# Chunked RWKV attention and a SwiGLU block in fp32: one masked score product per head for a 128-step chunk, and float64 weights rounded 768 columns at a time

## The chip, the cores and the metric

The kernel runs on one core of a Trainium2 chip. A core has TensorE (matrix products and turns, called PE in the profile, with its weight loads as PEld), VectorE (DVE), ScalarE (ACT), GpSimd (POOL) and SyncE (SP), which issues most transfers here. Each engine works through its own instructions in order and waits on the others by semaphores. The metric is the device time of one execution in microseconds; the time before is the median of three runs.

## The reference

Attention by linear recurrence per batch and head (4 batches, 8 heads, 768 steps, 48 columns per head), then a SwiGLU feed-forward block over 3072 tokens:

```python
for t in range(S):
    kt, vt, rt = (k[:, :, t], v[:, :, t], r[:, :, t])
    cur = np.einsum('bhd,bhe->bhde', u[None] * kt, vt)
    y[:, :, t] = np.einsum('bhd,bhde->bhe', rt, state + cur)
    state = w[None, :, :, None] * state + np.einsum('bhd,bhe->bhde', kt, vt)
...
x = y.transpose(0, 2, 1, 3).reshape(B * S, H * D)       # 3072 x 384
g = x @ w_gate                                           # 384 x 1536
silu = g * (1.0 / (1.0 + np.exp(-g)))
out = (silu * (x @ w_val)) @ w_out                       # 1536 x 384
```

`r`, `k`, `v` and `u` are fp32; `w` is `rand * 0.1 + 0.85`; the three weight matrices reach the kernel as float64, seen as int64.

## The kernel before

A unit is one chunk of 128 steps of one batch, with all 8 heads; there are 24 units, unit `i` being chunk `i // 4` of batch `i % 4`. In the turned layout the heads lie in pairs, head 2a+e on partitions 64e to 64e+47 of column a.

Three kinds of work are put in order by hand.

- **Attention.** `prepare(i)` turns k and r by TensorE (L211), copies them out of PSUM (L215), and multiplies the turned tiles by powers of w: for each of six levels l a key part on VectorE (L229) and a row part on GpSimd (L233), both into `sc`. It also forms `rhat` (L240, VectorE), `khat` (L224, GpSimd), `rk` (L220, L221), `du` (L243) and `dv` (L245). `scores(i)` splits the pairs (j, t) of a chunk by the highest bit in which j and t differ: seven levels, each with four products per half of the heads (L259, 64 columns wide) and one predicated copy into the score tile `At` under that level's mask (L265). No negative power of w occurs. `products(i)` multiplies scores by v (L282) and the old state by `rhat` (L277), forms the state's update `u_ps` (L290), adds `dv` to give `xs` (L297) and renews the state (L305 to L308). `turn_x(i)` turns `xs` for the block (L317, L318).
- **Weight rounding.** 36 chunks of 128 x 384 are loaded as float64 bits, three ahead (L115), and rounded to fp32 by integer operations: five on VectorE (L131, L134 to L137) and four on GpSimd (L132, L133, L138, L140).
- **The block.** 256 tokens (two units) form a group `g`, of which there are 12. `gate_value(g, f)` makes gate and value of 128 of the 1536 columns (L331), then sigmoid (L336, ScalarE) and two products (L337, L338, VectorE). `project(g, j)` multiplies by `w_out` (L344), copies (L349) and stores.

Group 0 rounds three weight chunks in each `gate_value`. A queue `todo` holds the block's items; the attention's step `s` feeds two of them after each of its four parts:

```python
for s in range(N + 2):
    if s < N:
        prepare(s)
        ...
        feed(2)
    if 1 <= s <= N:
        scores(s - 1)
        feed(2)
    if s >= 2:
        products(s - 2)
        feed(2)
        turn_x(s - 2)
        if s % 2:
            queue((s - 2) // 2)
        feed(2)
```

Of the kernel before, what the change touches and what calls it, by code (L numbers as in the profile page):

```python
# [10 lines left out]
INT32 = mybir.dt.int32  # L11
AF = mybir.ActivationFunctionType
ALU = mybir.AluOpType
AX = mybir.AxisListType
P = 128


@with_exitstack
def kernel(
    ctx: ExitStack,  # L20
# [11 lines left out]
    """RWKV5 in chunks of 128 steps, then the SwiGLU block, all in fp32.  # L32

    The weights of the block come as the bits of float64, in int64 tensors, and
    are rounded to fp32 on the chip.

    A unit is one chunk of one batch with its 8 heads. In the turned layout the
    heads lie in pairs, head 2a+e at partitions 64e..64e+47 of column a.

    Within a chunk, y_t takes r_t * w^(t-1-j) * k_j for j < t. The pairs (j, t)  # L40
    are split by the highest bit l in which j and t differ: there t is in an odd
    block of 2^l steps and j in the even one before it, and the exponent is
    (t mod 2^l) + (2^l - 1 - j mod 2^l). Both parts are at least 0, so no power
    of w is ever divided by, and any w will do.
    """
# [10 lines left out]
    ctx.enter_context(tc.manual_schedule())  # L56
# [40 lines left out]
    # chunk f of wg and wv: columns 128f.. of all CC row blocks; chunk f of wo: rows 128f..  # L97
# [82 lines left out]
    # masks[j, l, (m i)]: j is in the even block before the odd block m of t  # L180
# [14 lines left out]
    for t in state:  # L195
        pool.memset(t[:], 0.0)

# [1 line left out]
    turned, scaled, rhat, khat, dvs, xs, xT = {}, {}, {}, {}, {}, {}, {}  # L199

    def blocks(t, l):
# [215 lines left out]
```

## Time and profile before

| | |
|---|---|
| median of 3 runs | 1161.31 us (1160.63 to 1161.44) |
| span of the profiled execution | 1158.1 us |
| TensorE, products | 1025.8 us (89%), 5964 instructions |
| TensorE, weight loads | 868.1 us (75%) |
| VectorE | 591.4 us (51%) |
| GpSimd | 340.3 us (29%) |
| ScalarE | 106.7 us (9%) |
| mean granted TensorE clock | 0.860 |
| read from HBM, written | 28.51 MB, 4.72 MB |

The page is one profiled execution; its own time is its span of 1158.1 us, from its first to its last instruction. The median of the timed runs stands 3.2 us above it. A row of instructions names line, engine, operation, output and inputs, the shape, how many there were, the time in which any of them ran, the mean of one in ns, and the engine's idle time ahead of them with what ended it. A row of the chain of work that ended last, or of a timeline, gives start and duration in us; rows of equal kind are merged (xN). A row of the windows view gives, for a stretch, each engine's busy us and instructions (TensorE, its weight loads, VectorE, ScalarE, GpSimd), then the granted TensorE clock as a share of full speed, the share of the DMA engines and GB/s. Matrix products overlap each other, so the mean duration of one is longer than the distance between two starts.

### The profile page before, as it was taken

The numbers are of one execution on the slowest core, as the hardware profiler recorded it, in microseconds if no ns is written. First come the engines' busy times: TensorE is split into PE (matmuls) and PEld (weight loads), VectorE is DVE, ScalarE is ACT, GpSimd is POOL, SyncE is SP. The second block draws the span as 40 slices with busy tenths as digits, with TensorE's granted clock in tenths as the row PEclk, the third lists the DMA queues.
The fourth block names the chain that finished last, engine by engine and source line by source line (L and its number), as shares of the span: only waits on it lengthen the run. The fifth ranks groups of instructions, "written<-read, shape, count | busy, mean of one in ns | idle before, by whom it ended". The sixth has DMA issues, their size and how long they took to land.

```text
span 1158.1 us, 14858 instructions
## 1 busy us (share of the span) xinstructions
PE 1025.8 (89%) x5964; PEld 868.1 (75%) x5964; DVE 591.4 (51%) x1108; ACT 106.7 (9%) x243; POOL 340.3 (29%) x416
## 2 busy tenths in 40 slices
PE   3577335369999999999999999999999999999998
PEld 3577334257887987987987887887887888878875
DVE  7877989993353353354354344344434524522211
ACT  1001000000011011001100100100100100100110
POOL 9644857872113113113122221211311212100000
PEclk9999757667879879879879879879978978988999
DMA  5212323311011011011011001101101100000000
GB/s 136 55 41 48 89 69 96 95 35 28 8 21 28 8 21 28 8 22 35 1 22 35 18 5 35 21 1 35 22 1 35 22 1 14 1 7 8 1 14 14
DMA packets 90292, 34.18 MB, mean 30 GB/s; under 512 B 76272, under 2 KB 88688, under 8 KB 90224
## 3 DMA queue, kind: packets, MB, share of 16 engines
q1 hardware_dynamic: 90224, 33.24, 11.5%
q8 instruction: 47, 0.77, 0.3%
q14 instruction: 21, 0.17, 0.0%
HBM read 28.51 MB, written 4.72 MB: 29 GB/s over the span
## 4 chain that ended last, share of the span: by engine, by line
PE 74%; DVE 23%; issue 2%; ACT 1%; DMA 0%; SPq 0%; POOL 0%; ACTq 0%; DVEq 0%; POOLq 0%
PE gv L331 30%; PE s_ps L259 19%; PE o_ps L344 16%; DVE sc L229 6%; PE y_ps L282 4%; DVE w_mt L134 3%; DVE w_ex L131 3%; DVE w_mt L135 2%; PE u_ps L290 2%; PE y_ps L277 2%; DVE sg L337 1%; DVE w_mt L136 1%; DVE hT L338 1%; DVE rhat L240 1%; DVE w_up L137 1%
## 5 line engine op out<-in xcount | busy, mean ns | idle before, releaser
L259 PE MATMUL s_ps<-sc 48*128 48x64 f32 x2304 | 250.2, 367 | 64.0 <-DVE At L265 64.0
L331 PE MATMUL gv<-xT,wg 128*128 128x256 f32 x864 | 253.8, 437 | 55.9 <-POOL w_mt L138 39.8
L259 PEld LDWEIGHTS s_ps<-sc 48*128 48x128 f32 x2304 | 243.6, 271 | 66.2 <-DVE At L265 66.1
L331 PEld LDWEIGHTS gv<-xT,wg 128*128 128x128 f32 x864 | 182.2, 220 | 90.6 <-POOL w_mt L138 51.9
L331 PE MATMUL gv<-xT,wv 128*128 128x256 f32 x864 | 232.7, 410 | 0.0
L265 DVE COPY_PREDICATED At<-masks,s_ps 128x256 f32<-128x256 int32 x336 | 157.1, 530 | 124.3 <-PE s_ps L259 122.2
L337 DVE TENSOR_TENSOR sg<-sg,gv 128x256 f32<-128x256 f32 x144 | 60.3, 419 | 287.1 <-ACT sg L336 287.0
L331 PEld LDWEIGHTS gv<-xT,wv 128*128 128x128 f32 x864 | 182.8, 212 | 30.8
L344 PE MATMUL o_ps<-wo,hT 128*128 128x384 f32 x576 | 189.8, 486 | 0.6 <-ACT o_sb L349 0.6
L233 POOL TENSOR_TENSOR sc<-rT,up 128x256 f32<-128x256 f32 x144 | 124.0, 892 | 205.7 <-ACT rT L215 205.7
L344 PEld LDWEIGHTS o_ps<-wo,hT 128*128 128x128 f32 x576 | 109.4, 190 | 72.4 <-ACT o_sb L349 1.2
L229 DVE TENSOR_TENSOR sc<-kT,down 128x256 f32<-128x256 f32 x144 | 109.8, 828 | 70.8 <-ACT kT L215 70.8
L307 POOL TENSOR_TENSOR state<-state,wL 64x192 f32<-64x192 f32 x32 | 16.1, 502 | 366.6 <-PE y_ps L277 365.4
L336 ACT ACTIVATE sg<-gv 128x256 f32<-128x256 f32 x144 | 55.2, 383 | 719.5 <-PE gv L331 719.5
L338 DVE TENSOR_TENSOR hT<-sg,gv 128x256 f32<-128x256 f32 x144 | 60.6, 421 | 4.9
L282 PE MATMUL y_ps<-v_ld,At 128*128 128x48 f32 x384 | 58.4, 284 | 0.0
L282 PEld LDWEIGHTS y_ps<-v_ld,At 128*128 128x128 f32 x384 | 54.6, 209 | 0.4
L259 PEld LDWEIGHTS s_ps<-rT,kT 48*128 48x128 f32 x384 | 38.9, 204 | 10.3 <-issue 9.6
L259 PE MATMUL s_ps<-rT,kT 48*128 48x64 f32 x384 | 42.4, 294 | 0.0
L138 POOL TENSOR_TENSOR w_mt<-w_mt,w_ex 128x384 int32<-128x384 int32 x36 | 35.8, 993 | 19.0 <-DVE w_mt L136 18.8
L134 DVE TENSOR_SCALAR w_mt<-w_bits 128x384 int32<-128x384 int32 x36 | 37.1, 1030 | 0.0
L297 DVE TENSOR_TENSOR xs<-y_ps,dv 128x384 f32<-128x384 f32 x24 | 13.4, 557 | 43.5 <-PE y_ps L282 43.5
(57 smaller groups left out, 581.1 us busy)
## 6 DMA issues: line engine op xcount, KB each, us to landing
k_ld<-in_k_dram SPq DMA_DIRECT2D x24, 192.0 KB, 2.7
r_ld<-in_r_dram SPq DMA_DIRECT2D x24, 192.0 KB, 3.3
v_ld<-in_v_dram SPq DMA_DIRECT2D x24, 192.0 KB, 3.5
w_bits<-in_moe_w_gate_dram SPq DMA_DIRECT2D x12, 384.0 KB, 3.2
w_bits<-in_moe_w_val_dram SPq DMA_DIRECT2D x12, 384.0 KB, 3.3
w_bits<-in_moe_w_out_dram SPq DMA_DIRECT2D x12, 384.0 KB, 3.0
out_dram<-o_sb SPq DMA_DIRECT2D x24, 192.0 KB, 1.9
ub<-in_u_dram SPq DMA_DIRECT2D x1, 192.0 KB, 4.4
```

Source lines behind the costliest of these rows:

```text
L134: dve.tensor_scalar(mt[:], hi, 3, 0x7FFFF8, ALU.logical_shift_left, ALU.bitwise_and)
L138: pool.tensor_tensor(mt[:], mt[:], ex[:], ALU.add)
L229: dve.tensor_mul(blocks(x[:], l)[:, :, :, 0, :], blocks(kT[:], l)[:, :, :, 0, :], down[:, :, P - n : P].unsqueeze(2).to_broadcast([P, HP, ...
L233: pool.tensor_mul(blocks(x[:], l)[:, :, :, 1, :], blocks(rT[:], l)[:, :, :, 1, :], up[:, :, 0:n].unsqueeze(2).to_broadcast([P, HP, 64 // n ...
L259: pe.matmul(s_ps[:, a, :], keys[p0:p1, a, :], rows[p0:p1, a, :].rearrange("p (m o i) -> p m o i", o=2, i=n)[:, :, 1, :], start=True, stop= ...
L265: dve.copy_predicated(blocks(A[:, e], l)[:, :, :, 1, :], mask.unsqueeze(1).to_broadcast([P, HP, 64 // n, n]), s_ps[:].rearrange("p a (m i) ...
L282: pe.matmul(y_ps[:, a, D * e : D * (e + 1)], A[:, e, a, :], vl[:, 2 * a + e, :], start=(c == 0), stop=True, skip_group_check=True,)
L331: pe.matmul(gv[:, o, :], wt[:, c, P * f : P * (f + 1)], xT[g][:, c, :], start=(c == 0), stop=(c == CC - 1),)
L336: act.activation(sg[:], gv[:, 0, :], AF.Sigmoid)
L337: dve.tensor_mul(sg[:], sg[:], gv[:, 0, :])
L338: dve.tensor_mul(hT[g][:, f, :], sg[:], gv[:, 1, :])
L344: pe.matmul(o_ps[:], hT[g][:, f, P * j : P * (j + 1)], wo[:, f, :], start=(f == 0), stop=(f == FC - 1),)
```

## The change

A new program `fast` stands ahead of the old one, which is kept as `general` and runs only if a number that the chip counts itself, of decays w outside 0.8 to 1.25, is above zero.

In `fast`, k is multiplied by w^(127-j) and r by w^(-(128-t)) before the turn, in the layout in which they are loaded, on GpSimd; both factors are tables (`kscale`, `rscale`) made in the set-up with one reciprocal and eight turns. One product per head then gives all scores of a chunk, 128 columns wide over 48 rows (8 products per unit instead of 56), and one predicated copy per half of the heads (2 instead of 14) takes the part j < t. The six levels' scale products are gone; the turned `rT` also meets the state, which is now a block-diagonal tile `Z` with w^128 folded in (`wL`), updated whole. v is stored in a zero-padded tile, so that the two heads of a pair accumulate into the same 96 columns. Step `s` prepares unit s+1, turns unit s, takes the scores of unit s-1 and the outputs and update of unit s-2, and turns the outputs of unit s-3.

Weights are rounded in 18 chunks of 128 x 768: two operations on ScalarE, two on VectorE, one on GpSimd; one chunk after the turn of a step and one at its end. The block's queue is fed in six places of a step, with no items up to step 3, three per step in steps 4 to 7, six in 8 and 9, and twelve from 10; `project` is cut into three parts that lie between `gate_value` items. The output's store is issued by ScalarE. Cut to its core:

```diff
+W_LOW, W_HIGH = 0.8, 1.25
...
+    two = ctx.enter_context(tc.tile_pool(name="two", bufs=2))
+    three = ctx.enter_context(tc.tile_pool(name="three", bufs=3))
+    ps_a = ctx.enter_context(tc.tile_pool(name="ps_a", bufs=5, space=bass.MemoryType.PSUM))
+    ps_f = ctx.enter_context(tc.tile_pool(name="ps_f", bufs=2, space=bass.MemoryType.PSUM))
+    ps_o = ctx.enter_context(tc.tile_pool(name="ps_o", bufs=1, space=bass.MemoryType.PSUM))
...
+    v_ld = [cst.tile([P, HP, 2, 2 * D], FP32, name=f"v_ld{i}") for i in range(4)]
+    khat = [cst.tile([P, H, DP], FP32, name=f"khat{i}") for i in range(4)]
+    rhat = [cst.tile([P, H, DP], FP32, name=f"rhat{i}") for i in range(2)]
+    At = [cst.tile([P, 2, HP, P], FP32, name=f"At{i}") for i in range(2)]
+    def v_heads(i):
+        t = v_ld[i % 4]
+        return [t[:, :, e, D * e : D * (e + 1)] for e in range(2)]
...
+    def load_v(i):
+        c, b = divmod(i, B)
+        rows = slice(P * c, P * (c + 1))
+        for e, dst in enumerate(v_heads(i)):
+            sp.dma_start(
+                out=dst, in_=v[b, :, rows, :].rearrange("(a e) t d -> e t a d", e=2)[e]
+            )
...
+    chunks = []
+    for f in range(FC // 2):
+        for src, dst in ((moe_w_gate, wg), (moe_w_val, wv)):
+            cols = slice(2 * P * f, 2 * P * (f + 1))
+            chunks.append((src[:, cols].rearrange("(c p) f -> p c f", p=P), dst[:, :, cols]))
+    for f in range(FC // 2):
+        chunks.append((
+            moe_w_out[2 * P * f : 2 * P * (f + 1)].rearrange("(c p) f -> p c f", p=P),
+            wo[:, 2 * f : 2 * f + 2, :],
+        ))
+    WN = 6 * P
+    AHEAD = 3
...
+    def round_weights(count):
+        for _ in range(count):
+            n = state["rounded"]
+            if n == len(chunks):
+                return
+            state["rounded"] += 1
+            x = bits.pop(n)
+            lo, hi = x[:, :, 0], x[:, :, 1]
+            dst = chunks[n][1].bitcast(INT32)
+            mag = two.tile([P, WN], INT32, name="w_mag", tag="w_mag")
+            low = two.tile([P, WN], INT32, name="w_low", tag="w_low")
+            act.activation(mag[:].bitcast(FP32), hi.bitcast(FP32), AF.Abs, scale=float(2.0**-112))
+            act.activation(low[:], lo.bitcast(UINT32), AF.Copy, scale=float(2.0**-29))
+            c = dst.shape[1]
+            mag, low, hi = (t.rearrange("p (c f) -> p c f", c=c) for t in (mag[:], low[:], hi))
+            dve.tensor_scalar(dst, hi, -(1 << 31), None, ALU.bitwise_and)
+            dve.scalar_tensor_tensor(dst, mag, 3, dst, ALU.logical_shift_left, ALU.bitwise_or)
+            pool.tensor_tensor(dst, dst, low, ALU.add)
+            load_weights()
...
+    make_identity(nc, ident[:])
+    dve.tensor_scalar(held[:], wcol[:], W_LOW, W_HIGH, ALU.max, ALU.min)
+    dve.tensor_copy(sq[:, 0, :], held[:])
+    for l in range(1, 8):
+        dve.tensor_mul(sq[:, l, :], sq[:, l - 1, :], sq[:, l - 1, :])
+    pw = two.tile([P, HP, P + 1], FP32, name="pw", tag="hT")
+    ipw = two.tile([P, HP, P], FP32, name="ipw", tag="hT")
+    dve.memset(pw[:, :, P : P + 1], 1.0)
+    dve.tensor_copy(pw[:, :, P - 1 : P], held[:].unsqueeze(2))
+    for l in range(7):
+        n = 1 << l
+        f = sq[:, l, :].unsqueeze(2).to_broadcast([P, HP, n])
+        dve.tensor_mul(pw[:, :, P - 2 * n : P - n], pw[:, :, P - n : P], f)
+    dve.reciprocal(ipw[:], pw[:, :, 0:P])
+    for src, dst in ((pw[:, :, 1 : P + 1], kscale), (ipw[:], rscale)):
+        t_ps = ps_a.tile([P, HP, P], FP32, name="t_ps", tag="a")
+        for a in range(HP):
+            pe.transpose(t_ps[:, a, :], src[:, a, :], ident[:])
+        act.copy(dst[:].rearrange("p h d -> p (h d)"), t_ps[:].rearrange("p a x -> p (a x)"))
+    pool.memset(wL[:], 0.0)
+    for e in range(2):
+        q = slice(64 * e, 64 * e + 64)
+        dve.tensor_copy(
+            wL[q, :, D * e : D * (e + 1)], sq[q, 7, :].unsqueeze(2).to_broadcast([64, HP, D])
+        )
+    pool.memset(mask[:], 1.0)
+    pool.affine_select(
+        out=mask[:], in_=mask[:], compare_op=ALU.is_gt, fill=0.0,
+        base=0, pattern=[[1, P]], channel_multiplier=-1,
+    )
+    for t in At:
+        pool.memset(t[:], 0.0)
+    dve.tensor_tensor(bad[:], held[:], wcol[:], ALU.not_equal)
+    dve.tensor_reduce(badc[:], bad[:], axis=AX.X, op=ALU.add)
+    dve.memset(ones[:], 1.0)
+    n_ps = ps_a.tile([P, HP, P], FP32, name="n_ps", tag="a")
+    pe.matmul(n_ps[0:1, 0, 0:1], badc[:], ones[:], start=True, stop=True)
+    act.copy(outside, n_ps[0:1, 0, 0:1])
...
+    def prepare(i):
+        kl, rl = k_ld[i % 2], r_ld[i % 2]
+        rk = two.tile([P, H, D], FP32, name="rk", tag="rk")
+        pool.tensor_mul(khat[i % 4][:], kl[:], kscale[:])
+        pool.tensor_mul(rhat[i % 2][:], rl[:], rscale[:])
+        pool.tensor_mul(rk[:], rl[:, :, 0:D], kl[:, :, 0:D])
+        pool.tensor_mul(rk[:], rk[:], ub[:])
+        du = three.tile([P, H], FP32, name="du", tag="du")
+        dve.tensor_reduce(du[:], rk[:], axis=AX.X, op=ALU.add)
+        dus[i] = du
+        load_v(i)
+        if i + 2 < N:
+            load(i + 2)
+    def turn(i):
+        got = []
+        for nm, t in (("kT", khat[i % 4]), ("rT", rhat[i % 2])):
+            tp = ps_a.tile([P, HP, P], FP32, name="tp", tag="a")
+            for a in range(HP):
+                pe.transpose(
+                    tp[:, a, :], t[:, 2 * a : 2 * a + 2, :].rearrange("p e d -> p (e d)"), ident[:]
+                )
+            x = (two if nm == "kT" else three).tile([P, HP, P], FP32, name=nm, tag=nm)
+            act.copy(x[:], tp[:])
+            got.append(x)
+        turned[i] = got
+    def scores(i, e):
+        kT, rT = turned[i]
+        q = slice(64 * e, 64 * e + D)
+        ps = ps_a.tile([P, HP, P], FP32, name="s_ps", tag="a")
+        for a in range(HP):
+            pe.matmul(
+                ps[:, a, :], kT[q, a, :], rT[q, a, :],
+                start=True, stop=True, skip_group_check=True,
+            )
+        dve.copy_predicated(
+            At[i % 2][:, e], mask[:].bitcast(INT32).unsqueeze(1).to_broadcast([P, HP, P]), ps[:]
+        )
+    def own(i):
+        du = dus.pop(i)
+        dvs[i] = two.tile([P, HP, 2, D], FP32, name="dv", tag="dv")
+        for e, vh in enumerate(v_heads(i)):
+            dve.tensor_mul(
+                dvs[i][:, :, e, :], vh,
+                du[:].rearrange("p (a e) -> p a e", e=2)[:, :, e : e + 1].to_broadcast([P, HP, D]),
+            )
+    def outputs(i):
+        c, b = divmod(i, B)
+        A, vl = At[i % 2], v_ld[i % 4]
+        rT = turned.pop(i)[1]
+        ps = ps_a.tile([P, HP, 2 * D], FP32, name="y_ps", tag="a")
+        for a in range(HP):
+            if c > 0:
+                pe.matmul(
+                    ps[:, a, :], rT[:, a, :], Z[b][:, a, :],
+                    start=True, stop=False, skip_group_check=True,
+                )
+            for e in range(2):
+                pe.matmul(
+                    ps[:, a, :], A[:, e, a, :], vl[:, a, e, :],
+                    start=(c == 0 and e == 0), stop=(e == 1), skip_group_check=True,
+                )
+        xs[i] = two.tile([P, DM], FP32, name="xs", tag="xs")
+        dve.tensor_add(
+            xs[i][:], ps[:].rearrange("p a x -> p (a x)"),
+            dvs.pop(i)[:].rearrange("p a e d -> p (a e d)"),
+        )
+    def update(i):
+        c, b = divmod(i, B)
+        if c == NCH - 1:
+            return
+        kh, vl, z = khat[i % 4], v_ld[i % 4], Z[b]
+        ps = ps_a.tile([P, HP, 2 * D], FP32, name="u_ps", tag="a")
+        for a in range(HP):
+            pe.matmul(
+                ps[:, a, :].rearrange("p (e d) -> p e d", e=2),
+                kh[:, 2 * a : 2 * a + 2, :].rearrange("p e d -> p (e d)"),
+                bass.AP(
+                    tensor=vl.tensor, offset=vl[:, a, 0, :].offset,
+                    ap=[list(vl[:].ap[0]), [3 * D, 2], [1, D]],
+                ),
+                start=True, stop=True, skip_group_check=True,
+            )
+        if c == 0:
+            dve.tensor_mul(z[:], ps[:], wL[:])
+        else:
+            dve.tensor_add(z[:], ps[:], z[:])
+            pool.tensor_mul(z[:], z[:], wL[:])
+    def turn_x(i):
+        tp = ps_a.tile([P, CC, P], FP32, name="xtp", tag="a")
+        x = xs.pop(i)
+        for c in range(CC):
+            pe.transpose(tp[:, c, :], x[:, P * c : P * (c + 1)], ident[:])
+        act.copy(xT[:, i % NX, :, :], tp[:])
...
+    def gate_value(g, f):
+        if g == 0:
+            round_weights(2 * (f // 2) + 4 - state["rounded"])
...
+    def project(g, j, part):
+        c, b = divmod(2 * g + j, B)
+        round_weights(len(chunks) - state["rounded"])
+        if part == 0:
+            o_ps[g, j] = ps_o.tile([P, DM], FP32, name="o_ps", tag="o")
+        ps = o_ps[g, j]
+        for f in range(4 * part, 4 * part + 4):
+            pe.matmul(
+                ps[:], hT[g][:, f, P * j : P * (j + 1)], wo[:, f, :],
+                start=(f == 0), stop=(f == FC - 1),
+            )
+        if part == 2:
+            o_sb = two.tile([P, DM], FP32, name="o_sb", tag="o_sb")
+            act.copy(o_sb[:], ps[:])
+            n0 = S * b + P * c
+            act.dma_start(out=out[n0 : n0 + P, :], in_=o_sb[:])
...
+    def queue(g):
+        for f in range(FC):
+            todo.append(lambda g=g, f=f: gate_value(g, f))
+            if g > 0 and f >= 2 and f < 8:
+                todo.append(lambda g=g, n=f - 2: project(g - 1, n // 3, n % 3))
+    prepare(0)
+    for s in range(N + 3):
+        per = [0] * 6 if s < 4 else [1, 0, 1, 0, 1, 0] if s < 8 else [1] * 6 if s < 10 else [2] * 6
+        if s + 1 < N:
+            prepare(s + 1)
+        if s < N:
+            turn(s)
+        round_weights(1 if s else 0)
+        feed(per[0])
+        if 1 <= s <= N:
+            scores(s - 1, 0)
+            feed(per[1])
+            scores(s - 1, 1)
+            own(s - 1)
+            feed(per[2])
+        if s >= 3:
+            turn_x(s - 3)
+            if s % 2 == 0:
+                queue((s - 4) // 2)
+            feed(per[3])
+        if 2 <= s <= N + 1:
+            outputs(s - 2)
+            feed(per[4])
+            update(s - 2)
+        round_weights(1 if s > 1 else 0)
+        feed(per[5])
+    feed(len(todo))
+    for j in range(2):
+        for part in range(3):
+            project(N // 2 - 1, j, part)
...
 def tile_rwkv5_eagle__then__ffn_swiglu_block_kernel(
+    ctx: ExitStack,
+    tc: tile.TileContext,
+    *args: bass.AP,
+):
+    nc = tc.nc
+    ctx.enter_context(tc.manual_schedule())
+    flag = ctx.enter_context(tc.tile_pool(name="flag", bufs=1))
+    outside = flag.tile([1, 1], INT32, name="outside")
+    fast(tc, *args, outside[:])
+    n = nc.values_load(outside[:], min_val=0, max_val=512)
+    with tc.If(n > 0):
+        general(tc, *args)
+@with_exitstack
+def general(
```

More of the change, by code (lines that the diff above doesn't have):

```diff
@@ L11 @@
 INT32 = mybir.dt.int32
+UINT32 = mybir.dt.uint32
 AF = mybir.ActivationFunctionType
@@ L18 @@
 @with_exitstack
 def kernel(
+    ctx: ExitStack,
+    tc: tile.TileContext,
+    *args: bass.AP,
+):
+    nc = tc.nc
+    ctx.enter_context(tc.manual_schedule())
[5 more added lines that the diff above has]
+        general(tc, *args)
+@with_exitstack
+def general(
     ctx: ExitStack,
@@ L54 @@
     NL = 7
-    ctx.enter_context(tc.manual_schedule())
     cst = ctx.enter_context(tc.tile_pool(name="cst", bufs=1))
```

93 lines of the change are left out of this document (added).

## The prediction

> **What bounds the kernel now.** I read the page first (busy shares, the slices, the chain), then the chain in order of time, then the busy time by windows, and last the timelines of TensorE, VectorE and GpSimd.
>
> ```profile
> span 1158.1 us, 14858 instructions
> PE   3577335369999999999999999999999999999998
> DVE  7877989993353353354354344344434524522211
> PE 74%; DVE 23%; issue 2%; ACT 1%; DMA 0%; SPq 0%; POOL 0%; ACTq 0%; DVEq 0%; POOLq 0%
> ```
>
> Two stages. Up to slice 9 (some 255 us) VectorE is full and TensorE is not; from there TensorE is full to the end. The first product of the block starts late, at 105.9 us, and until about 250 us each waits for rounded weights.
>
> ```profile
> L331 PE MATMUL gv<-xT,wg x864: 379/379/797, 105.9 to 1136.8; 128*128 128x256 f32 x173
> ```
>
> The chain in order of time gives the second stage. Every source-level fp32 product is two instructions (864 are listed for 432 in the source); transposes are one.
>
> ```profile
> 303.62 6.94 PE gv L331 x24
> 314.11 5.21 PE gv L331 x24
> 366.16 0.87 PE tp L211 x8
> 367.04 2.59 PE gv L331 x12
> 369.63 7.74 PE o_ps L344 x24
> 377.37 10.07 PE s_ps L259 x112
> 387.44 7.69 PE gv L331 x24
> 419.09 9.03 PE s_ps L259 x72
> ```
>
> From 303.62 to 387.44 two units pass: 83.8 us. Two units hold 12 products of `gv` (2.59 each where undisturbed, so 31.1), two of `o_ps` (15.5), two rounds of scores (10.07 in one, over 9 in the other) and the small rest. The 24 instructions of `gv` take 5.21 us, but 6.9 to 7.7 behind scores. The granted clock says why:
>
> ```profile
> 400.00:410.00 10.00, 10.00 (x53) 8.82 (x53) 2.68 (x7) 2.04 (x6) 1.87 (x2) 1.00 0.00 0
> 420.00:430.00 10.00, 10.00 (x73) 9.52 (x73) 4.84 (x12) 0.00 (x0) 0.00 (x0) 0.50 0.00 0
> core 0: 1158.1 us, clock 0.860
> ```
>
> It is 1.00 in products and falls to 0.50 in the scores (420 to 430 us), so scores cost their own time and about 2 us of the products behind.
>
> **The change part by part: TensorE.** Scores go from 56 source products of 64 columns per unit to 8 of 128 columns. No row has 48 rows by 128 columns in fp32. Half of `gv`'s 2.59/12 = 0.216 us for 256 columns is 0.108; the wide score rows of before are 9.03/72 = 0.125 at half clock. So 16 instructions cost 1.7 us, or 2.0 at the upper end; I take 1.73. The two transposes now turn the already scaled k and r, at the same 0.87.
>
> ```profile
> 310.56 0.19 PE y_ps L277 x2
> 313.18 0.93 PE u_ps L290 x8
> 319.32 0.33 PE xtp L317 x3
> 355.03 0.49 ACT xT L318
> ```
>
> `y_ps` becomes 96 columns wide over a zero-padded v. The state product is already 96 wide, and 24 instructions from 310.56 to 313.18 take 0.109 each, as does `u_ps` at 96 columns (0.93/8 = 0.116), so width costs 0 to 16 x 0.007 = 0.1 us; I take 2.62 unchanged. A unit then takes 0.87 + 1.73 + 2.62 + 0.93 + 0.33 = 6.48, against some 14 to 15 with the scores of before.
>
> All of TensorE at full clock: 144 `gv` x 2.59 = 373.0; 24 `o_ps` x 7.74 = 185.8 (split in three parts each, same instructions); 24 units x 6.48 = 155.5, less 4 first chunks without a state product (8 x 0.109 each, 3.5) and 4 last chunks without an update (3.7), 148.3. Sum 707.1 us. Two units then take 31.1 + 15.5 + 13.0 = 59.6 instead of 83.8. That is 8.2 per unit fewer in scores and about 2 from the clock; the rest of the difference is the stalls around score evacuation, which go with the seven rounds.
>
> Does the clock stay up? The row 400 to 410 says so for products; the new order puts two queued items (5.2 us) between each small group, and none of the groups between them (0.87, 0.87, 0.87, 2.62, 0.93) is as long as the scores that pulled it down. The Trainium skill, "TensorE: Matmul & The Clock Gate", Part 4, states that transposes do not count as busy for the clock; the rows at 366 and 367 us show a transposition group of 0.87 followed by products at the full 2.59, which neither confirms nor excludes it for longer groups.
>
> **VectorE, GpSimd, ScalarE: the rounding.**
>
> ```profile
> 105.50 0.36 DVE L131 TENSOR_SCALAR w_ex<-w_bits 128x384 int32<-128x384 int32 x1
> 107.87 1.17 DVE L131 TENSOR_SCALAR w_ex<-w_bits 128x384 int32<-128x384 int32 x1
> 110.15 0.75 DVE L135 SCALAR_TENSOR_TENSOR w_mt<-w_bits,w_mt 128x384 int32<-128x384 int32 x1
> 111.87 1.17 DVE L131 TENSOR_SCALAR w_ex<-w_bits 128x384 int32<-128x384 int32 x1
> 107.82 0.99 POOL L138 TENSOR_TENSOR w_mt<-w_mt,w_ex 128x384 int32<-128x384 int32 x1 [0.55 <-DVE w_mt L136]
> 108.89 1.01 POOL L140 TENSOR_TENSOR wg<-w_mt,w_up 128x384 int32<-128x384 int32 x1
> ```
>
> A chunk of 384 columns takes 107.87 to 111.87 = 4.0 us, VectorE's five operations and GpSimd's four. `TENSOR_SCALAR` is 0.36 alone and 1.17 when it starts beside a GpSimd operation of 1.0: one waits for the other. The change leaves, for 768 columns, one such operation (0.36 to 0.72 alone, up to 2.3 beside the add; 0.6 taken), one scalar-tensor-tensor (0.75 to 1.5; 1.3), one GpSimd add (1.0 to 2.0; 2.0) and two on ScalarE.
>
> ```profile
> L336 ACT ACTIVATE sg<-gv 128x256 f32<-128x256 f32 x144 | 55.2, 383 | 719.5 <-PE gv L331 719.5
> L215 ACT COPY rT<-tp 128x512 f32<-128x512 f32 x24 | 14.2, 591 | 1.3 <-PE tp L211 1.1 <-ACT kT L215 0.2
> L224 POOL TENSOR_TENSOR khat<-k_ld,downt 128x512 f32<-128x512 f32 x20 | 26.4, 1319 | 13.0 <-PE u_ps L290 13.0
> L220 POOL TENSOR_TENSOR rk<-r_ld,k_ld 128x384 f32<-128x384 f32 x24 | 25.3, 1055 | 1.3
> L243 DVE TENSOR_REDUCE du<-rk 128x8 f32<-128x384 f32 x24 | 12.9, 539 | 0.0
> L221 POOL TENSOR_TENSOR rk<-rk,ub 128x384 f32<-128x384 f32 x24 | 24.2, 1010 | 1.9
> L265 DVE COPY_PREDICATED At<-masks,s_ps x336: 410/443/781, 33.3 to 1048.1; 128x256 f32<-128x256 int32 x168
> L337 DVE TENSOR_TENSOR sg<-sg,gv 128x256 f32<-128x256 f32 x144 | 60.3, 419 | 287.1 <-ACT sg L336 287.0
> L297 DVE TENSOR_TENSOR xs<-y_ps,dv 128x384 f32<-128x384 f32 x24 | 13.4, 557 | 43.5 <-PE y_ps L282 43.5
> ```
>
> ScalarE: 0.383 for 256 columns and 0.591 for 512 make 0.8 for 768; two per chunk, 29 us in all, on an engine whose waits for `gv` alone come to 719.5: hidden, since they wait only for the load; if not, 1.6 per chunk. Table loads may be added; hidden likewise.
>
> Now one step `s` early on. GpSimd's `prepare`: khat and rhat 1.32 each (rhat moves here from VectorE), rk 1.06 + 1.0 = 4.7. VectorE, in order: du 0.54 (waits for rk), rounding 1.9, two predicated copies (0.44 for 256 columns, some 0.7 for 512; the six scale products and twelve of fourteen copies go), two parts of dv 0.35 each (192 columns, from 0.42 for 256), xs 0.56, state 0.56, rounding 1.9; GpSimd adds 2.0 after each. VectorE's in-order wait for rk is a new serial link: the next `prepare` stands behind the second add. One step is 4.7 + 0.54 + 1.9 + 3.3 + 1.9 + 2.0 = 14.3; I add 0.7 for the mutual waits: 15. Bounds: 9 if the queues overlap fully (GpSimd's own 4.7 + 4.0), 20 if every operation stands behind the other engine's.
>
> ```profile
> 10.41 2.50 DVE sc L229 x3
> 1146.80 8.02 PE o_ps L344 x24
> ```
>
> Set-up: the first scale product of before starts at 10.41; the reciprocal and seven power products replace fourteen, so 10 for `prepare(0)` (9 to 15, the reciprocal over 512 columns has no row). Two prepares to 19.4; s=1 (one chunk) to 28.5; s=2, 3, 4 at 15 to 73.5, with the first `gv` at some 64 instead of 105.9. Steps 5 to 7 carry three `gv` each, six more VectorE products of 0.42 = 2.5: 17.5 each, to 126. By then TensorE has done 7 units (45) and 10 `gv` (26), 71 us. From s=8 it has 15.5 us and more of queued items per step beside 6.5 of attention, more than 15 to 20 of the others: it is the bound.
>
> **Loads.**
>
> ```profile
> w_bits<-in_moe_w_gate_dram SPq DMA_DIRECT2D x12, 384.0 KB, 3.2
> out_dram<-o_sb SPq DMA_DIRECT2D x24, 192.0 KB, 1.9
> 10.00:15.00 5.00, 5.00 (x27) 4.61 (x25) 4.59 (x5) 2.14 (x4) 4.92 (x7) 1.00 0.72 232
> ```
>
> A 768 KB chunk at 232 GB/s is 3.4 us (6.4 at twice the landing time shown); a step of two chunks and 576 KB of k, r, v is 9.3, under 15, three chunks ahead: nothing. v is fetched in two transfers, issued behind the product work of `prepare` and ahead of k and r of the unit after next: one more issue per unit on SP, which loses the output's. That one moves to ScalarE, behind the copy it stores: the next sigmoid waits for it, hidden by the second `gv` buffer, or half a us each time where it is not.
>
> **Sum.** 126 + (707 - 71) = 762. Where the queue has run short (from about s=18, and in each even step) `gv` directly follows the turn of x and waits 0.5 for ScalarE (row 355.03); 12 such, and as much again for buffers: 10. After the last product (1146.80 + 8.02) come copy and store: 1158.1 less 1154.8 is 3.3. Span 775. The median of 1161.31 is 3.2 above the span: 778.5. The value read at the end and the branch on five engines are unseen: 0 if behind the last store (1.9), 5 as two fetches with a landing like 3.2 or less; I take 2. **780 us.** On that branch, "Runtime: NRT & Kernel Launch", section Instruction fetch mechanics, of the Trainium skill states that a taken branch out of the fetched window must fetch its target; no run here shows it, and it stands inside those 5 us.
>
> **Rivals.** (a) Rounding still holds the start: if TENSOR_SCALAR always meets an add (2.3) and steps take 20, step 8 begins at 28.5 + 3 x 20 + 3 x 22.5 = 156 instead of 126: 810; one more such step would make 827. Against it: VectorE loses most of its other work. (b) The clock falls in the new order too. With the mean of before (0.86) over the 636 us left, 636/0.86 = 740, so 104 more: 884. For it: 48-row products stay; against: they are 1.7 us per step in two pieces. The mechanism: turn and scores are 0.87 + 1.73 = 2.6 us of light work per step, and the long scores show what such work does to the clock. The page of the Trainium skill named above, by which turns do not count, would make it likelier. (c) The start overlaps fully: steps of 9 to 54 us, then TensorE's own 6.5 + 7.8 for three steps, so step 8 begins at 97, 29 earlier: 751. Against it: VectorE's queue holds `du` in order before the rounding. (d) The other side: the count of decays outside 0.8 to 1.25 is not zero, and the general program runs after the fast one: 780 + 1158 = 1938. It decides at one w out of range; the reference draws 0.85 to 0.95 and padding is 1.0, so it should not. (e) No change: TensorE would have to stand idle 380 us more, 16 in each of 24 steps, which takes each step's chain of 15 being added to TensorE's 30 rather than lying beside it: about 1160. The stalls of before, at most 0.6 per `gv`, speak against it.
>
> **How the numbers follow.** Forecast 0.66 (760 to 800), (a) 0.13, (b) 0.09, (c) 0.09, (d) 0.02, (e) 0.01. The range holds the forecast, (a) and (c) with their bounds: 748 to 828; outside stay (b), (d), (e). Less than 0.2% (2.3 us) cannot be told from no change: faster 0.97, same 0.01, slower 0.02.
>
> **What the next profile shows.** Right: score instructions of 128 columns x384, about 0.11 us apart; chain nearly all TensorE after 126 us; clock 1.00 from there; two units in about 60 us; first `gv` near 64 us. Wrong: clock 0.5 in steady windows (b); TensorE waiting for VectorE or GpSimd beyond 140 us (a); instructions on lines of the general program (d); a gap between the last store and the span's end above 5 us.

## The result: 1161.28 us before, 794.97 after

The changed kernel takes 794.97 us (median of 4, 792.4 to 795.47) against 1161.28 (median of 4): a ratio of 0.6845, 95% interval 0.6834 to 0.6856. The forecast was 780, with a range from 748 to 828.

The page of the profile after, the lines that answer to those of before:

```profile
span 793.2 us, 8984 instructions
PE   3878888999999999999999999999999999999996
DVE  5554565633222323222223223223223123212120
PEclk9958898999999999999999999999999999999999
PE 81%; DVE 8%; POOL 8%; issue 2%; ACT 1%; DMA 0%; SPq 0%; POOLq 0%; DVEq 0%
```

TensorE is full from the eighth slice (139 us) instead of the tenth, longer one (261 us), and from there the clock is at 9 tenths or more. VectorE, which was full in the first stage, is busy for about half of it.

The chain in order of time, around two pairs of units:

```profile
498.80 2.62 PE gv L333 x12
...
516.10 1.08 PE s_ps L254 x8
517.19 2.79 PE gv L333 x12
...
548.44 0.87 PE tp L241 x8
549.32 1.64 PE s_ps L254 x16
...
552.00 5.45 PE gv L333 x24
...
560.10 2.62 PE gv L333 x12
```

Two units take 560.10 - 498.80 = 61.3 us; they took about 84. Scores are two groups of eight instructions, 1.08 us each, or sixteen in a row where the queue is empty, and no product of this stage runs at half speed: the 24 behind scores and the turn of x take 5.45 (it was 6.9 to 7.7). The windows view gives the clock as 1.00 over the middle:

```profile
200.00:400.00 200.00, 200.00 (x982) 160.53 (x982) 53.16 (x120) 26.76 (x63) 27.04 (x25) 1.00 0.10 21
```

The start, in GpSimd's timeline (the khat product opens a step's `prepare`; its four rows open steps 3, 4, 5 and 8), and the first product of the block:

```profile
44.73 1.28 POOL L225 TENSOR_TENSOR khat<-k_ld,kscale 128x512 f32<-128x512 f32 x1
58.97 1.27 POOL L225 TENSOR_TENSOR khat<-k_ld,kscale 128x512 f32<-128x512 f32 x1
73.99 1.26 POOL L225 TENSOR_TENSOR khat<-k_ld,kscale 128x512 f32<-128x512 f32 x1
127.54 1.26 POOL L225 TENSOR_TENSOR khat<-k_ld,kscale 128x512 f32<-128x512 f32 x1
L333 PE MATMUL gv<-xT,wg x864: 379/379/767, 60.6 to 769.7; 128*128 128x256 f32 x173
```

Steps 3 and 4 take 14.2 and 15.0 us, and step 8 opens at 127.5. Groups of the lines view show the new operations (busy, mean ns, then idle before):

```profile
L254 PE MATMUL s_ps<-rT,kT 48*128 48x128 f32 x384 | 54.4, 310 | 2.2 <-DVE At L258 2.2
L258 DVE COPY_PREDICATED At<-mask,s_ps 128x512 f32<-128x512 int32 x48 | 33.5, 726 | 42.5 <-PE s_ps L254 42.3
L151 ACT ACTIVATE w_mag<-w_bits 128x768 f32<-128x768 f32 x18 | 16.5, 917 | 2.3 <-DVE wg L156 1.0 <-DVE wv L156 0.9 <-DVE wo L156 0.3
L155 DVE TENSOR_SCALAR wg<-w_bits 128x768 int32<-128x768 int32 x6 | 5.6, 940 | 0.0
L156 DVE SCALAR_TENSOR_TENSOR wg<-w_mag,wg 128x768 int32<-128x768 int32 x6 | 5.8, 958 | 0.6
L157 POOL TENSOR_TENSOR wg<-wg,w_low 128x768 int32<-128x768 int32 x6 | 10.9, 1810 | 23.2 <-DVE wg L156 9.6 <-ACT w_mag L151 9.3 <-ACT sg L339 4.3
```

### The profile page after: what moved, and what is told of

Same layout as the page of the kernel before. It is cut to its first block, busy times and chain, and to the rows that moved or that the text cites. A ratio compares the mean times of both kernels' runs of the same rounds, so it can differ in the third digit from the quotient of the medians.

```text
span 793.2 us, 8984 instructions
## 1 busy us (share of the span) xinstructions
PE 749.0 (94%) x3666; PEld 604.1 (76%) x3666; DVE 250.3 (32%) x520; ACT 137.0 (17%) x281; POOL 159.0 (20%) x142
## 4 chain that ended last, share of the span: by engine, by line
PE 81%; DVE 8%; POOL 8%; issue 2%; ACT 1%; DMA 0%; SPq 0%; POOLq 0%; DVEq 0%
PE gv L333 45%; PE o_ps L352 22%; PE s_ps L254 4%; PE y_ps L283 4%; PE y_ps L278 2%; POOL khat L225 2%; POOL rhat L226 2%; PE tp L241 2%; DVE wo L156 1%; PE u_ps L300 1%; POOL rk L228 1%; POOL rk L227 1%; POOL wg L157 1%; PE xtp L319 1%; DVE wg L156 1%
## 5 line engine op out<-in xcount | busy, mean ns | idle before, releaser
L333 PE MATMUL gv<-xT,wg 128*128 128x256 f32 x864 | 217.6, 388 | 13.8 <-DVE hT L341 11.5
L333 PEld LDWEIGHTS gv<-xT,wg 128*128 128x128 f32 x864 | 158.1, 192 | 38.8 <-issue 11.5
L283 PE MATMUL y_ps<-v_ld,At 128*128 128x96 f32 x384 | 61.7, 293 | 0.7 <-issue 0.7
L254 PE MATMUL s_ps<-rT,kT 48*128 48x128 f32 x384 | 54.4, 310 | 2.2 <-DVE At L258 2.2
L258 DVE COPY_PREDICATED At<-mask,s_ps 128x512 f32<-128x512 int32 x48 | 33.5, 726 | 42.5 <-PE s_ps L254 42.3
L225 POOL TENSOR_TENSOR khat<-k_ld,kscale 128x512 f32<-128x512 f32 x24 | 30.5, 1272 | 6.2 <-ACT kscale L195 6.2
L226 POOL TENSOR_TENSOR rhat<-r_ld,rscale 128x512 f32<-128x512 f32 x24 | 30.5, 1272 | 2.1 <-ACT outside L217 2.1
L278 PE MATMUL y_ps<-Z,rT 128*128 128x96 f32 x160 | 30.4, 271 | 0.0
L278 PEld LDWEIGHTS y_ps<-Z,rT 128*128 128x128 f32 x160 | 25.7, 192 | 3.1
L300 PEld LDWEIGHTS u_ps<-v_ld,khat 128*128 128x128 f32 x160 | 23.2, 211 | 2.7
```

The source lines that it names most:

```text
L225: pool.tensor_mul(khat[i % 4][:], kl[:], kscale[:])
L226: pool.tensor_mul(rhat[i % 2][:], rl[:], rscale[:])
L254: pe.matmul(ps[:, a, :], kT[q, a, :], rT[q, a, :], start=True, stop=True, skip_group_check=True,)
L258: dve.copy_predicated(At[i % 2][:, e], mask[:].bitcast(INT32).unsqueeze(1).to_broadcast([P, HP, P]), ps[:])
L278: pe.matmul(ps[:, a, :], rT[:, a, :], Z[b][:, a, :], start=True, stop=False, skip_group_check=True,)
L283: pe.matmul(ps[:, a, :], A[:, e, a, :], vl[:, a, e, :], start=(c == 0 and e == 0), stop=(e == 1), skip_group_check=True,)
```

## The experiments

Two theories carried the prediction: after some 130 us TensorE is the bound at full clock, and before that each step is a serial chain of VectorE and GpSimd. Their rivals were the clock, the engines' mutual waits and a hidden cost in the 48-row products. All kernels below are edits of the changed kernel, but for two of the kernel before. The ratios are to runs of the kernel before that were timed beside them, with medians of 1160.5 to 1160.9 us.

### What the scores cost: `full_rows` and `pair`

In `full_rows` the score products read both heads' rows; the scores are then the sums of a pair.

```diff
-                ps[:, a, :], kT[q, a, :], rT[q, a, :],
+                ps[:, a, :], kT[:, a, :], rT[:, a, :],
```

> The score products read all 128 rows of both turned tiles instead of the 48 rows of one head, in the same number of instructions and columns, so both heads of a pair get the sum of the two scores. Theory (the cost above 0.108 us per instruction comes from the switch between 48-row and 128-row products): 8 scores take 0.87 us, the product behind 2.59, and the time falls by 15 to 20 us. Rival (it comes from the weight loads or from the 128 columns themselves): 1.08 and 2.79 as before, within 3 us of 795.

786.43 us, ratio to before 0.6777 (0.6765 to 0.6788), 8.5 less than the changed kernel. The chain in order of time:

```profile
255.86 0.89 PE s_ps L254 x8
256.75 5.18 PE gv L333 x24
262.83 2.59 PE gv L333 x12
```

Eight instructions take 0.89, and the products behind them run at their plain 2.59. The 0.19 within the group and the 0.20 behind it are the price of changing between 48 and 128 rows: 0.78 per unit with two groups. The starts of the single instructions in the two traces show that the change costs this and not the 48 rows as such: inside a group they are 0.112 apart in both kernels, and only four gaps, two at each end of the group, are longer, by some 0.1 each. The whole gain is 8.5, about half of what was expected. It is what 11 units make and not 24: of the 15 units whose scores come after 175 us, when TensorE is the bound, 11 have two groups, and in the other four the queue is empty and the sixteen stand together anyway.

In `pair` the two halves stand together:

```diff
             scores(s - 1, 0)
-            feed(per[1])
             scores(s - 1, 1)
+            feed(per[1])
```

> Both halves of the scores are issued one behind the other, with the queue's items after both instead of between them. Theory (a group of 48-row products costs a change on each side: 8 alone take 1.08 us and lengthen the product behind by 0.2, 16 in a row take 1.64 and 0.25): 0.6 to 0.7 us less per unit, 10 to 16 us in all. Rival (the time goes with the instructions, not with the changes): within 3 us of 795; if the longer group pulls the clock down, above it.

787.59 us, 0.6785 (0.6773 to 0.6796), 7.4 less. Sixteen in a row:

```profile
257.64 1.64 PE s_ps L254 x16
259.28 7.97 PE gv L333 x36
```

1.64 + 0.2 (7.97 against 3 x 2.59) instead of 2 x 1.28 is 0.72 less per unit. Only 0.39 of it is a change saved. The rest is overlap: sixteen take less than two undisturbed groups of `full_rows` (2 x 0.89), because the second half begins 0.005 us behind the fifth instruction of the first, and three starts of each half fall together within that. The halves read different rows (0 to 47 and 64 to 111); that this lets them overlap is likely, but no run tests it. The direction and the price per unit were as expected, the total lower than the 10 to 16, for the same reason as in `full_rows`. The clock does not fall over 1.64 us of such products: the windows view has 1.00 from 200 to 780 us.

### The chain of an early step: `du_late`, `both_first`, `spread`, `best_demand`

`du_late` moves VectorE's sum over rk from `prepare` to behind the first rounding:

```diff
     def prepare(i):
         ...
-        dve.tensor_reduce(du[:], rk[:], axis=AX.X, op=ALU.add)
         ...
         round_weights(1 if s else 0)
+        if s + 1 < N:
+            sums(s + 1)
         feed(per[0])
```

> The sum du of the next unit, for which VectorE waits on GpSimd's second rk product, is issued after the first rounding of the step instead of before it. Theory (the in-order wait for rk is a serial link of each early step, 15 us apart in the profile): the two rounding operations run beside GpSimd's 4.5 us of products, a step falls from 15 to 12 to 13, and the time by 6 to 15 us. Rival (TensorE at lowered clock sets these steps, or the pairs of engines exclude each other at SBUF so that nothing overlaps): within 3 us of 795.

782.38 us, 0.6742 (0.673 to 0.6753), 12.6 less, as the theory had it. In GpSimd's timeline a step is now 53.36 - 41.01 = 12.35 us, and the cost of overlap shows:

```profile
41.01 1.98 POOL L225 TENSOR_TENSOR khat<-k_ld,kscale 128x512 f32<-128x512 f32 x1
...
53.36 2.00 POOL L225 TENSOR_TENSOR khat<-k_ld,kscale 128x512 f32<-128x512 f32 x1
```

The khat product that now meets VectorE's rounding takes 1.98 instead of 1.28. VectorE's scalar-tensor-tensor beside it, at 52.42 us, takes 1.81 instead of 0.96. The engines do hold each other up, by 0.7 us here. One wait, moved within VectorE's order, gained more than `full_rows` or `pair`.

`both_first` puts both roundings of a step there:

```diff
-        round_weights(1 if s else 0)
+        round_weights(0 if s == 0 else 1 if s == 1 else 2)
         ...
-        round_weights(1 if s > 1 else 0)
         feed(per[5])
```

> Both roundings of a step stand before the sum du, so VectorE rounds beside GpSimd's products of prepare, and GpSimd adds beside VectorE's copies, dv and xs. Theory (the chain of the step is what counts): steps of 12.4 to 13.2 with du alone moved fall to 9 to 11, the time from 782 to 768 to 776. Rival (the two engines shut each other out at SBUF, so rounding beside the products gains nothing more): 779 to 785.

768.69 us, 0.6617 (0.66 to 0.6634), 26.3 less than the changed kernel, at the lower end of what the theory expected. What limits the step now stands in VectorE's timeline of the kernel `best`, further below, which has the same order:

```profile
46.14 2.24 DVE L271 TENSOR_TENSOR dv<-v_ld,du 128x192 f32<-128x192 f32 x2
...
50.28 1.30 DVE L156 SCALAR_TENSOR_TENSOR wv<-w_mag,wv 128x768 int32<-128x768 int32 x1
...
52.55 1.78 DVE L156 SCALAR_TENSOR_TENSOR wg<-w_mag,wg 128x768 int32<-128x768 int32 x1
...
55.97 2.24 DVE L271 TENSOR_TENSOR dv<-v_ld,du 128x192 f32<-128x192 f32 x2
```

From dv to dv, one step, are 9.83 us, and the operations of VectorE and of GpSimd in that step each add up to about 10: both engines are full. The pair of dv products takes 2.24 beside GpSimd's adds (0.61 in step 8 of the changed kernel), the scalar-tensor-tensor 1.30 to 1.78 instead of 0.96.

`spread` rounds earlier and only on demand, to take the burst of four chunks out of step 8:

```diff
-        round_weights(1 if s else 0)
+        round_weights(1)
         feed(per[0])
         ...
-        round_weights(1 if s > 1 else 0)
+        round_weights(1 if s else 0)
         ...
-        round_weights(len(chunks) - state["rounded"])
+        round_weights(FC + 2 * part + 2 - state["rounded"])
```

> One chunk more is rounded in step 0 and one more in step 1, and a part of project asks only for the chunks that it reads, so no step rounds more than two chunks from step 2 on. Theory (start is bound by the chain of VectorE and GpSimd in each step, the burst of four chunks in step 8 lies beside TensorE's products): 0 to 3 us less than the 795 of the changed kernel. Rival (the burst in step 8, in which VectorE rounds from 149.5 to 160.6 us, is what made the prediction 15 us too low): 8 to 12 us less.

803.37 us, 0.6916 (0.6899 to 0.6932): 8.4 more. Both expectations were wrong in sign. The two early roundings lengthened the first steps and delayed the first product:

```profile
L333 PE MATMUL gv<-xT,wg x864: 379/379/767, 69.7 to 778.1; 128*128 128x256 f32 x173
```

It starts at 69.7 instead of 60.6, 9.1 us later, and the end is 8.2 later in span; between the two times of this row, 69.7 to 778.1 and 60.6 to 769.7, the two kernels differ by less than 1 us. Steps are a chain, so a chunk put into a light step costs as much as in a heavy one; the burst cost less than that. `best_demand` takes the on-demand edit alone, on top of the best kernel below:

> As the one before, and a part of project asks only for the chunks that it reads, so the burst of three forced roundings in step 8 goes. Theory (the burst lies beside queued products): within 2 us of the one before. Rival (it costs): 3 to 6 less.

766.76 us, 0.6603 (0.6587 to 0.6619), 5.8 more than `best`, which neither theory nor rival expected. TensorE's timeline has the reason:

```profile
137.12 1.46 PE L357 MATMUL o_ps<-wo,hT 128*128 128x384 f32 x4
141.81 2.92 PE L357 MATMUL o_ps<-wo,hT 128*128 128x384 f32 x4 [3.24 <-POOL wo L157]
```

The part of `project` now stands in TensorE's order directly behind the rounding that it asked for, waits 3.24 us for GpSimd's add, and comes back at half speed (2.92 for what takes 1.3 to 1.5). Rounding all at once, one step ahead of use, is what keeps these weights off the path.

### The rounding's share: `old_rounding`, `one_op`, `before_new_rounding`

`old_rounding` puts the arithmetic of before on the new chunks:

```diff
-            act.activation(mag..., AF.Abs, ...); act.activation(low..., AF.Copy, ...)
-            dve.tensor_scalar(dst, hi, -(1 << 31), None, ALU.bitwise_and)
-            dve.scalar_tensor_tensor(dst, mag, 3, dst, ...)
-            pool.tensor_tensor(dst, dst, low, ALU.add)
+            # the five VectorE and four GpSimd operations of before, on 768 columns
```

> The changed kernel with the rounding arithmetic of before (five operations on VectorE, four on GpSimd) on its chunks of 768 columns; its products, order and loads stay. Theory (the rounding's share of the gain is the length of the early steps): a chunk costs 7 to 8 us of VectorE and GpSimd in series instead of 3.7, two per step make a step 22 to 25 us instead of 15 to 18, and the time rises by 50 to 70 us to 845 to 865. Rival (the rounding is hidden in either form, the gain is the scores' alone): within 10 us of 795.

865.76 us, 0.7456 (0.7443 to 0.7468), 70.8 more, just above the 50 to 70 expected. `before_new_rounding` is the other side, the new arithmetic alone in the kernel before, on its chunks of 384:

> The kernel before with only the new rounding arithmetic (two operations on ScalarE, two on VectorE, one on GpSimd) on its own chunks of 384 columns. Theory (its first 255 us are set by VectorE's and GpSimd's rounding and scale products, the rest by TensorE): 36 chunks at 4.0 us become some 2.0, 60 to 75 us less, 1085 to 1100. Rival (the start is bound by the scale products and scores): less than 30 us.

1082.74 us, 0.9326 (0.931 to 0.9342), 78.1 less, more than the 60 to 75 expected. So the rounding is worth 70 to 80 us in either kernel, and the rest of the change 295.1 (1160.85 - 865.76), with the old rounding kept. How these 295 divide among fewer score instructions, the clock and the new order no run separates. `one_op` shows what rounding still costs:

```diff
-            (the five operations)
+            act.activation(dst, hi, AF.Abs, scale=float(2.0**-112))
```

> Rounding is left out but for one ScalarE operation per chunk on the upper words (the weights are then wrong); VectorE and GpSimd round nothing. Theory (early steps are the chain of both engines): a step falls from 15 to the attention's own 7 to 10 us until TensorE binds, the time by 25 to 40 us to 755 to 770. Rival (TensorE's low clock or the loads set the early steps): less than 10 us.

761.72 us, 0.6558 (0.6547 to 0.6569), 33.3 less, within the 25 to 40 expected; it leaves four of the five operations out, so its weights are not usable. The start of the changed kernel was bound by the chain; with the rounding gone TensorE is all but full from the second slice (19 us):

```profile
PE   2989999999999999999999999999999999999997
```

### The clock: `before_scores_spread`

The kernel before, with the queue's items between the levels of the scores and none elsewhere but behind the turn of x:

```diff
     def scores(i):
+        per = [1, 1, 1, 1, 1, 1, 0]
         ...
+            feed(per[l])
...
-            feed(2)
         if 1 <= s <= N:
             scores(s - 1)
-            feed(2)
         if s >= 2:
             products(s - 2)
-            feed(2)
             turn_x(s - 2)
```

> The kernel before with the queue's items put between the levels of the scores (one after each of six levels, two after the turn of the outputs); nothing else. Theory (long runs of 48-row products pull the clock to 0.50; runs of 16 between two products do not): mean clock from 0.860 to 0.95, the products behind scores back to 2.59, time 25 to 60 us less. Rival (such products pull the clock down in any arrangement, or what is saved is lost to switches between 48 and 128 rows at 0.4 us per run, 7 runs per unit, 67 us): the same 1161 or more.

1145.5 us, 0.9859 (0.9808 to 0.991): some 15 less, with single runs from 1137 to 1150, which is under 2% and short of the 25 to 60 expected. The mean clock is 0.885; the runs of the kernel before beside it have 0.816 to 0.845. Both theories hold in part. The chain in order of time, twice the same work:

```profile
408.88 1.53 PE s_ps L260 x16
410.41 2.79 PE gv L333 x12
413.20 1.53 PE s_ps L260 x16
414.73 2.79 PE gv L333 x12
417.52 3.54 PE s_ps L260 x48
...
428.00 5.17 PE gv L333 x12
...
501.81 3.54 PE s_ps L260 x48
...
509.98 2.86 PE gv L333 x12
```

```profile
410.00:420.00 10.00, 10.00 (x82) 8.68 (x81) 4.72 (x13) 0.77 (x2) 0.00 (x0) 1.00 0.00 0
420.00:430.00 10.00, 9.43 (x54) 8.59 (x53) 2.62 (x7) 0.48 (x1) 4.22 (x5) 0.62 0.01 2
510.00:520.00 10.00, 10.00 (x35) 6.74 (x36) 0.84 (x2) 0.38 (x1) 2.22 (x2) 1.00 0.00 1
```

Where products of the block stand between the levels, the clock is 1.00 through the runs of sixteen. Where the queue had run dry, the last three levels stay together (48 instructions) and outputs, update and turn of x follow without a product of the block. At 417.5 the clock then falls, to 0.62 in the next window, and a group of products takes 5.17 instead of 2.59; at 501.8 the same stretch leaves it at 1.00. The clock records of the traces tell how often, after 250 us. Stretches of 8.2 us like these lowered the clock in four cases of nine; those of 5.5 us, with 16 scores ahead of the outputs, in three of ten. One fall came at 1064.2, after 4.0 us of outputs with a wait of 0.6 in them. In the kernel before, the scores of a unit, 9.3 to 12.9 us as they ran, lowered it every time; in the changed kernel, where no stretch after 140 us is longer than 3.7 us, it never fell. So the falls go with the length of an unbroken stretch of light work, scores or others, and not with the number of scores; from 4 to 9 us the length alone does not decide, and what does is not shown. The separate runs each pay their change of rows (2.79 for 2.59), which returns part of the gain.

### The branch: `no_branch`

```diff
-    n = nc.values_load(outside[:], min_val=0, max_val=512)
-    with tc.If(n > 0):
-        general(tc, *args)
```

> The count is still made, but nothing reads it, there is no branch, and the general program is left out. Theory (five engines read one value and jump at the end, after the last store was issued): 0 to 4 us less than 795, at the end of the span; 2 was put into the prediction. Rival (nothing, the store of the last tile covers it): within 1 us.

790.98 us (790.85 to 794.29), 0.6826 (0.6813 to 0.6839), against 0.6845 (0.6834 to 0.6856). The medians differ by 4.0, but the intervals overlap, and in the profiles 2.3 us of it lies ahead of the end of the last product, which the edit does not touch. The timelines end so, the changed kernel first:

```profile
788.22 0.34 ACTq L360 DMA_DIRECT2D out_dram<-o_sb  x1
```

```profile
785.91 0.34 ACTq L360 DMA_DIRECT2D out_dram<-o_sb  x1
```

From there to the end of the span are 793.2 - 788.22 = 5.0 and 789.2 - 785.91 = 3.3 us. The branch costs some 1.7 us in these two profiles. The other traces bear it out: in ten kernels with the branch the span ends 4.3 to 5.0 us after this issue, without it 3.3, so the branch takes 1.1 to 1.7 us. By the medians alone no more than that it is small can be told.

### A faster version: `best`

`both_first` and `pair` together.

> Both roundings first, and the two score halves one behind the other. Theory (the gains lie in different stages and add up): 7 us less than with both roundings first alone, 761 to 769. Rival (the pair's gain came from the start): no more than 2 less.

760.95 us (759.73 to 761.49), 0.6552 (0.6541 to 0.6562): 34 us less than the changed kernel, 7.7 less than `both_first`, and as fast as that kernel with its rounding all but left out. The gains of the two edits add up (26.3 + 7.4 = 33.7), as two stages would have it.

## Why the prediction was right, and where it was 15 us short

**The early step.** The chain of 14.3 + 0.7 was right in its sum (14.2 to 15.0 between khat products) and in its reason: `du_late` takes VectorE's wait for rk out of the order and the step falls to 12.35. That the sum came out so well is in part luck, since its terms were off against each other: scalar-tensor-tensor 0.96 and not 1.3 (on `wo`, mostly beside GpSimd's add, 1.88 in the mean), tensor-scalar 0.94 (0.55 on `wo`) and not 0.6, the add 1.8 and not 2.0. The first product came at 60.6 (64 forecast), step 8 at 127.5 (126).

**What TensorE had done by then.** The prediction credited TensorE with 71 us of its work at 126, so 55 us of waiting. Counted by the changed kernel's order and at the prediction's own prices, the work ahead of step 8 is 10 products of gv (25.9), 8 turns, 7 scores, 6 outputs (4 of them without state) and updates, 5 turns of x: 64.4 us. "7 units" at the full 6.48 was 6.5 too much, since early units have no state product and the later steps of a unit lag behind. TensorE, which runs ahead of GpSimd, was through with it at 122.7, when it turned unit 8; so 58.3 us had gone without such work, 3.3 more than forecast.

**Steps 8 and 9.** The prediction had TensorE as the bound from here. It was not yet. VectorE's and TensorE's timelines:

```profile
132.09 0.55 DVE L230 TENSOR_REDUCE du<-rk 128x8 f32<-128x384 f32 x1 [6.46 <-POOL rk L228]
134.54 0.42 DVE L341 TENSOR_TENSOR hT<-sg,gv 128x256 f32<-128x256 f32 x1
136.89 0.61 DVE L266 TENSOR_TENSOR dv<-v_ld,du 128x192 f32<-128x192 f32 x2
135.10 2.15 PE L333 MATMUL gv<-xT,wg 128*128 128x256 f32 x6 [3.81 <-DVE hT L341]
168.58 1.53 PE L333 MATMUL gv<-xT,wg 128*128 128x256 f32 x6 [0.54 <-DVE hT L341]
```

VectorE waits 6.46 for rk, and the products of `hT` stand behind that and a rounding: 3.8 us of TensorE's time. The prediction had named this link, but ended it at step 8. After the wait the clock is down (0.66 between 135 and 140 us), and the chain gives these twelve products 4.51 instead of 2.59. From the turn of unit 8 to that of unit 10, at 174.7, the order holds 44.1 us of work at the prediction's prices, and 52.0 passed. The 7.9 between are the wait (3.8), the half speed behind it (1.9), two units of scores dearer than forecast (1.7) and a second wait (0.5). The last stands at the end of the chain through the burst of four roundings, and is all that the two timelines show the burst to cost TensorE. Together with the 3.3 these are 11 of the 15 us.

**The steady stage.** TensorE at full clock was right (1.00), and so were the other small terms: 0.87 for the turns, 2.66 for the outputs (2.62 forecast), 0.86 for the update (0.93). Of the 707.1 us, 598.6 were left at 174.7; to the last product's end at 787.7 it takes 613.0. That is 14.4 more, where the prediction had put 10 for stalls. The mis-sized term is the scores: 1.73 per unit were 2 x (1.08 + 0.20) = 2.56 where they stand in two groups, 9 us over the 11 units of this stage; `full_rows` gave back 8.5. The prediction proportioned a 48-row product to a 128-row one and had no row for the change between them, and its upper end of 2.0 was too low. The stalls, on the other hand, are small in the waits view (total, times, longest):

```profile
PE gv L333 <- ACT xT L320: 2.3, 4, 0.6
```

Instead of 10 us there are two or three. That the two errors nearly cancel is luck; what is left is 4.

**The end.** From the last product (779.67 + 8.02) to the time of the profiled run (794.99) are 7.3 us; 3.3 + 3.2 + 2 = 8.5 was forecast. The branch, 2 within bounds of 0 to 5, is 1.1 to 1.7 by the profiles. So 11.2 + 4.4 - 1.2 is 14.4, and the forecast's own terms add up to 780.5: together 795.

**The rivals.** (b) fell: no window of the middle is below 1.00. The Trainium skill, "TensorE: Matmul & The Clock Gate", Part 4, states that turns do not count as busy in the same way as products. Here that changed nothing: 0.87 us of turns and 1.64 of scores in a row (548.44 to 550.96), with the turn of x behind them, left the next 24 products at 5.45, that is, at full clock. Whether the turns were counted no run here shows. (a) and (c) are now edits: `old_rounding` is a start that rounding holds (865.8), `one_op` one that it does not (761.7; (c) forecast 751, from a start of 54 us for which its own steps of 9 behind 28.5 give 55.5). (d) did not occur: no instruction on a line of the general program is in the trace. (e), no change, is out by the time itself.

## What to carry to other kernels

Where several in-order engines hand work around in a step, write the step as a chain and look for an early wait that holds later independent work: moving one reduction behind the rounding gained more than the row changes of all scores cost. Before spreading a burst of preparation, see whether it already lies ahead of its use: put off until the use, it became a wait. Keep stretches without heavy products short enough for the clock, but do not cut light products into more runs than that needs: one run of 16 instructions per unit beat two of 8, because it pays one change of rows less and its halves overlap.

## What the runs showed of the hardware that was not expected

A change between 48-row and 128-row products costs TensorE about 0.2 us on each side (0.89 to 1.08 within eight, 2.59 to 2.79 behind them). Two groups of 48-row products on different rows, one behind the other, ran in part side by side (16 in 1.64 us, against 1.78 for 16 with 128 rows). Stretches without a product of the block lowered the clock each time at 9.3 us and more, in 7 cases of 19 at 5.5 and 8.2, and never at 3.7 and less in the changed kernel after 140 us. VectorE's two-input operations pay for GpSimd's presence: a pair of 192-column products takes 0.61 us, or 2.24 beside GpSimd's adds, and GpSimd's khat product 1.28, or 1.98 beside VectorE's rounding. And the reciprocal of the set-up, which had no row before, takes 3.35 us for 512 columns in VectorE's timeline:

```profile
8.32 3.35 DVE L190 RECIPROCAL ipw<-pw 128x512 f32<-128x512 f32 x1
```
